# Two groups of one unit in place of one group of two, ahead of the seven-product groups of a linear-attention and bilinear-FFN kernel

## The chip, the cores and the metric

The kernel runs on one core of a Trainium2 chip. The metric is the device time of one execution in microseconds, lower is better. Four executions of the kernel before took 224.36, 224.94, 225.21 and 227.12 us; their median is 225.07 us.

## The reference

Attention with decay, causal, in blocks, for 4 batches of 8 heads, 768 positions and 64 channels; its output, with the heads side by side, is the input x (3072 x 512) of a feed-forward layer without an activation:

```python
intra = np.einsum('bhic,bhjc->bhij', qb, kb) * Dmask[None]     # lam ** (i - j) for i >= j
intra = np.einsum('bhij,bhjd->bhid', intra, vb)
inter = np.einsum('bhid,bhde->bhie', qb * lam_pow[None], kv_state)
out[:, :, sl] = intra + inter
kv_state = lam_block * kv_state + np.einsum('bhsd,bhse->bhde', kb_dec, vb)
...
a = x @ w_a                     # 512 -> 1536
b = x @ w_b
return (a * b @ w_out)          # 1536 -> 512
```

## The kernel before

**Units.** A unit is 128 positions of one batch with all heads; there are 24, six to a batch. For each unit the kernel scales q and k by powers of lam (`make_qs`, `make_ks`, so that the decay becomes a plain triangular mask), brings both into transposed form, makes the scores on TensorE and masks them on VectorE (`piece_S`, two mask operations of 128x512), adds v's outer products into a running state in PSUM and copies it out (`piece_V`, or `kv_beside` within `pieces_O`), and multiplies state and masked scores into the attention output, which ScalarE copies into the group's `xT` (`pieces_O`, lines 401 to 421).

**Groups.** The feed-forward layer runs over groups of units: `GROUPS = (4, 2, 4, 4, 4, 4, 2)`. Groups 0 and 1 use `ffn` (line 617): for each of 12 column blocks f, four matmuls into an a bank, a ScalarE copy, four matmuls into a b bank, and a VectorE product into `ab`; then 12 matmuls a unit with `wo_sb`, 512 wide. The moving operand of an a or b matmul is as wide as the group, 128 columns a unit. The groups in `S_GROUPS` (2 to 6) use `ffn_seven` (line 484): two by two blocks with seven products for eight, in six pairs of column blocks (i = 0 to 5; three fours in the last group). It needs sums of `xT` (`sums`, lines 468 to 480, on VectorE) and of the weights (`w_sums`, lines 459 to 466, "TW" in the plan, 24 VectorE operations in group 0). Of each pair, the sum `c11` goes to VectorE (line 532) where the pair is in `SUM_ON_VEC`, else to GpSimd (line 535); GpSimd always makes the product of the first half (line 545).

**Order.** The order on each engine is written by hand. While group g's feed-forward layer runs, `PLAN[g]` says at which slot the attention of later units is put in: "P" scales q and k of a unit, starts its DMA transposition (units 6 and later) and lets further q and k loads be issued on SyncE's queue (`prep_k`, `pump`); "T" transposes on TensorE (units 4 and 5); "S", "V", "O" and "O2" are the pieces above, for one or two units. Slots 0 to 11 follow the column blocks f; in group 0 each later slot follows two output matmuls, in group 1 six. In `ffn_seven`, slots are spread over the 42 steps in the same order. Engines run apart from one another and wait only for data and for buffers, so a slot fixes the order on an engine, not the time.

**Buffers.** Seven PSUM banks are handed out in turn (`ps_bank`); a matmul that starts a bank waits for the last reader of the bank's earlier content. In the output part of group 0, four are held. The k of units 4 to 9 is scaled on VectorE, everything else on GpSimd (line 260).

**Loads.** The weights come on GpSimd's queue, with the cast to bf16, and so does v (`make_vb`). v of units 4 and 5 is issued between the chunks of `w_out` (lines 761 and 762); v of a later unit is issued behind that unit's "P" (line 803). q and k of units 4 and 5 go on SyncE's queue behind small DMAs that read chunks 0 and 3 of `w_out`, and so wait for them (line 163). The outputs of the rows in the first `KEEP_GROUPS` groups (units 0 to 5) are kept in SBUF and stored in a later group ("W").

Of the kernel before, what the change touches and what calls it, by code (L numbers as in the profile page):

```python
# [22 lines left out]
def _bc(ap, dims):  # L23
# [1 line left out]
    return dataclasses.replace(ap, ap=dims)  # L25


GROUPS = (4, 2, 4, 4, 4, 4, 2)
W_CHUNKS = (256,) * 6
W_STEPS = ((0, 1), (2,), (3,), (4, 5))  # L30
W_HALVES = (4, 5)
DMA_T = range(6, 24)
KEEP_GROUPS = 2
PACK = 4


# [1 line left out]

S_GROUPS = (2, 3, 4, 5, 6)
SUM_ON_VEC = {2: (0, 1, 2, 3, 4), 3: (2, 3, 4), 4: (2, 3, 4), 5: (1, 2, 3, 4), 6: (0, 1, 2)}
PLAN = {
    0: [(0, "V", 3), (4, "TW", 0), (6, "TW", 1), (9, "TW", 2), (11, "TW", 3), (14, "TW", 4),
        (18, "TW", 5), (23, "P", 4), (26, "T", 4), (27, "P", 5), (28, "S", 4), (30, "T", 5),
        (31, "V", 4), (32, "S", 5), (34, "O2", (4, 5)), (35, "P", 6)],
    1: [(1, "P", 7), (3, "P", 8), (6, "P", 9), (7, "S", 6), (8, "V", 6), (9, "S", 7), (11, "O2", (6, 7)),
        (12, "S", 8), (12, "V", 8), (13, "S", 9), (13, "P", 10), (14, "O2", (8, 9)), (15, "P", 11)],
    2: [(1, "P", 12), (4, "P", 13), (7, "P", 14), (11, "S", 10), (11, "S", 11), (12, "P", 15),
        (14, "P", 16), (17, "P", 17)],  # L50
    3: [(6, "P", 18), (9, "P", 19), (13, "P", 20), (16, "P", 21)],
    4: [(6, "P", 22), (9, "P", 23)],
    5: [(11, "V", 22), (13, "O2", (22, 23))],
}
for _g, _u in ((2, 10), (3, 14), (4, 18)):
    PLAN[_g] += [(11, "V", _u), (13, "Q", (_u, _u + 1, _u + 2, _u + 3)), (14, "V", _u + 2),
                 (16, "O2", (_u + 2, _u + 3)), (18, "S", _u + 4), (19, "S", _u + 5)]
PLAN[2] += [(_s, "W", None) for _s in (9, 9, 9, 10, 10, 10)]


@with_exitstack
def kernel(
# [12 lines left out]
    B, H, S, D = q.shape  # L75
# [5 lines left out]
    NU = B * NB  # L81
    assert sum(GROUPS) == NU and GROUPS[0] == PACK
    KS = d_model // 128
# [60 lines left out]
    def load_w(kind, c):  # L144
        if kind == "o":
            nc.gpsimd.dma_start(out=wo_sb[:, 2 * c:2 * c + 2, :], in_=wo_r[:, 2 * c:2 * c + 2, :])
        else:
            nc.gpsimd.dma_start(out=w_part(wa_sb if kind == "a" else wb_sb, c),
                                in_=w_part(wa_r if kind == "a" else wb_r, c))

    n0 = GROUPS[0]
    pending = [("after", 0), ("q", n0), ("k", n0), ("after", 3), ("q", n0 + 1), ("k", n0 + 1), ("after", 5)]
# [100 lines left out]
    def make_vb(u):  # L253
        b, nb = divmod(u, NB)
        vb = prep_pool.tile([128, H, D], BF16, name="vb", tag="vb", bufs=8)
        nc.gpsimd.dma_start(out=vb, in_=vr[b, nb])  # L256
        U.setdefault(u, {})["vb"] = vb

    def prep_k(u):
        make_ks(u, "dve" if u < n0 + 6 else "pool")  # L260
        make_qs(u, "pool")
        used["u"] = u + 1
        if u in DMA_T:
            qkT = qkT_pool.tile([128, 2, HP, 128], BF16, name="qkT", tag="qkT")
            nc.sync.dma_start_transpose(
                out=qkT[:].rearrange("p j hp i -> p (j hp) i"),
                in_=U[u]["qk"][:].rearrange("p j h d -> p (j h d)"))
            U[u]["qT"], U[u]["kT"] = qkT[:, 0], qkT[:, 1]
        pump()

    def piece_T(u):
        d = U[u]
        tps = ps_bank("tps", [128, 2, HP, 128], BF16)
        for j in range(2):
            for hp in range(HP):
                nc.tensor.transpose(tps[:, j, hp, :], d["qk"][:, j, 2 * hp:2 * hp + 2, :], ident)
        qkT = qkT_pool.tile([128, 2, HP, 128], BF16, name="qkT", tag="qkT")
        nc.scalar.copy(qkT, tps)
        d["qT"], d["kT"] = qkT[:, 0], qkT[:, 1]
# [110 lines left out]
    def piece_S(u):  # L390
        masks(u, scores(u))

    def piece_V(u):
        kv_update(u)
        if u % NB < NB - 1:
            kv_copy(u, kv["ps"])
# [26 lines left out]

    g_u0 = [sum(GROUPS[:i]) for i in range(len(GROUPS))]
    out_r = out.rearrange("(t p) n -> t p n", p=128)
# [33 lines left out]
    def w_sums(i):  # L459
        t = tw[i] = wst_pool.tile([128, 4, 2, 256], BF16, name="tw", tag="wst")  # L460
        c = slice(256 * i, 256 * i + 256)
        a1, a2, b1, b2 = wa_sb[:, 0:2, c], wa_sb[:, 2:4, c], wb_sb[:, 0:2, c], wb_sb[:, 2:4, c]
        nc.vector.tensor_sub(t[:, 0], b1, a1)
        nc.vector.tensor_sub(t[:, 1], b2, t[:, 0])
        nc.vector.tensor_sub(t[:, 2], b2, b1)
        nc.vector.tensor_sub(t[:, 3], a2, t[:, 1])

    def sums(u):
        g = next(i for i in range(len(GROUPS)) if g_u0[i] <= u < g_u0[i] + GROUPS[i])
        if g not in S_GROUPS or u != g_u0[g] + GROUPS[g] - 1:  # L470
            return
        h = GROUPS[g] * BLK // 2
        x = xTs[u][0]
        t = wst_pool.tile([128, 4, 2, h], BF16, name="xs", tag="wst")
        x11, x12, x21, x22 = (x[:, k:k + 2, c:c + h] for c in (0, h) for k in (0, 2))
        nc.vector.tensor_add(t[:, 0], x22, x21)
        nc.vector.tensor_sub(t[:, 1], t[:, 0], x11)  # L477
        nc.vector.tensor_sub(t[:, 2], x11, x21)
        nc.vector.tensor_sub(t[:, 3], x12, t[:, 1])
        xs[g] = t  # L480

    tw, xs = {}, {}

    def ffn_seven(g, u0, n, xT, hook, last):
        h = n * BLK // 2
        nf = 512 // h
# [29 lines left out]
        def step(i, n):  # L516
# [10 lines left out]
            elif n == 2:  # L527
                p, pb = bank_of("m_p")
                product(i, p, w_of(wa_sb, 2, i), x12, True)
                d["c11"] = a_pool.tile([128, nf, h], BF16, name="c11", tag="a")  # L530
                if i in SUM_ON_VEC[g]:
                    nc.vector.tensor_add(d["c11"], d["s12"][:, 0], p)  # L532
# [28 lines left out]
        for s in range(end):  # L561
            if s in at:
                step(*at[s])
            if s % 7 == 1 and s < 42:
                hook(2 * (s // 7))
            if s % 7 == 4 and s < 35:
                hook(2 * (s // 7) + 1)
# [22 lines left out]
    def store_kept():  # L590
        row, o_sb = kept.pop(0)
        nc.sync.dma_start(out=out_r[row], in_=o_sb)

    def store(row, op, lo, hi, queue=None):
        if row < g_u0[KEEP_GROUPS]:
            if row % 2 == 0:
                keep["t"] = wst_pool.tile([128, 2, d_model], F32, name="o_kept", tag="wst")
            o_sb = keep["t"][:, row % 2, :]
            nc.scalar.copy(o_sb, op)
            kept.append((row, o_sb))  # L600
            return
        o_sb = o_pool.tile([128, d_model], F32, name="o_sb", tag="osb")
        nc.scalar.copy(o_sb[:, lo:hi], op[:, lo:hi])  # L603
        (queue or nc.sync).dma_start(out=out_r[row][:, lo:hi], in_=o_sb[:, lo:hi])
# [49 lines left out]
    def new_xT(g):  # L654
        gx[g] = xT_pool.tile([128, KS, 512], BF16, name="xT", tag="xT")
        for i in range(GROUPS[g]):
            xTs[g_u0[g] + i] = (gx[g], i * BLK)
# [100 lines left out]
                load_w(kind, c)  # L758
    for c in range(FC // 2):
        load_w("o", c)  # L760
        if c in (3, 5):
            make_vb(n0 + (c - 3) // 2)
    for u in range(2):
        kv_part(u, (0, 1))
    for u in range(2):
# [25 lines left out]
    for g, n in enumerate(GROUPS):  # L791
        if g + 1 < len(GROUPS):
            new_xT(g + 1)
        plan = {}
        for slot, name, us in PLAN.get(g, ()):
            plan.setdefault(slot, []).append((name, us))

        def hook(slot, plan=plan):
            for name, us in plan.get(slot, ()):
                if name == "P":  # L800
                    prep_k(us)
                    if us > n0 + 1:
                        make_vb(us)
                elif name == "TW":
                    w_sums(us)
                elif name == "W":
                    store_kept()
                elif name == "T":
                    piece_T(us)
                elif name == "S":  # L810
                    piece_S(us)
                elif name == "V":
                    piece_V(us)
                elif name == "O":
                    pieces_O((us,))
                elif name == "O2":
                    pieces_O(us)
                else:
                    pieces_O(us[:2], us[2:])

        if g in S_GROUPS:
            ffn_seven(g, g_u0[g], n, gx.pop(g), hook, g + 1 == len(GROUPS))
        else:
            ffn(g_u0[g], n, gx.pop(g), hook, g == 0)
# [29 lines left out]
```

## Time and profile before

The profiled execution took 224.36 us, of which the span of the core's instructions is 222.7 us. TensorE's granted clock was 1.00 throughout.

| Part of the trace | from, us | to, us |
|---|---|---|
| Loads, attention of units 0 to 3 | 0 | 17.7 |
| Group 0, column blocks | 17.7 | 38.7 |
| Group 0, output matmuls, attention of units 4 and 5 | 38.7 | 53.6 |
| Group 1 (units 4 and 5), attention of units 6 to 9 | 53.6 | 73.9 |
| Groups 2 to 5, seven products | 73.9 | 204.9 |
| Group 6 | 204.9 | 222.7 |

| Engine | busy, us | share of the span |
|---|---|---|
| TensorE (PE) | 215.0 | 97% |
| VectorE (DVE) | 146.0 | 66% |
| GpSimd (POOL) | 117.2 | 53% |
| ScalarE (ACT) | 99.7 | 45% |

A row of the timeline gives the start and the length in microseconds, the engine, the line, the operation, what is written and read, the shape, and how many were merged; in brackets stands how long the engine was idle before, and what ended that. A merged row of matmuls ends when the last one's result is out, so consecutive rows overlap; the time that TensorE really spends is read from start to start. The output rows of the page's DMA part give the median time from a DMA's issue to its landing: 5.0 us for v, 4.4 and 4.9 us for q and k, 10.2 us for a chunk of `w_out`.

### The profile page before, as it was taken

How to read it: one execution, taken by the hardware profiler on the slowest of the kernel's cores; microseconds unless marked ns; L12 is line 12 of the kernel's file. 1: busy time of each engine (PE TensorE's matmuls, PEld its weight loads, DVE VectorE, ACT ScalarE, POOL GpSimd, SP SyncE). 2: the span in 40 equal slices, each digit the busy share in tenths (PEclk: the TensorE clock that was granted, in tenths of full speed). 3: DMA queues.
4: the chain of work that ended last, by engine and by line, in shares of the span. 5: the costliest groups of instructions: out<-in, count | busy, mean ns of one | idle time of the engine just before them, and what ended most of it. 6: DMA issues, size and time to landing. Idle time of an engine off the chain costs nothing.

```text
span 222.7 us, 5228 instructions
## 1 busy us (share of the span) xinstructions
PE 215.0 (97%) x2099; PEld 146.4 (66%) x2099; DVE 146.0 (66%) x250; ACT 99.7 (45%) x182; POOL 117.2 (53%) x131
## 2 busy tenths in 40 slices
PE   7799999989999999999999999999999999999994
PEld 2475444445874788754788754788744688745974
DVE  0991685975786788893678773578773598730760
ACT  3685233028432655324556324556324556332622
POOL 6689451057346579894269992269920144600230
PEclk9999999999999999999999999999999999999999
DMA  4999999999999999999960999300911200012102
GB/s 133 267 131 172 197 205 197 199 214 199 212 222 211 206 240 107 265 288 251 238 164 18 182 219 220 121 4 17 123 51 47 97 1 3 0 47 97 47 3 94
DMA packets 98606, 31.79 MB, mean 143 GB/s; under 512 B 86551, under 2 KB 95639, under 8 KB 98583
## 3 DMA queue, kind: packets, MB, share of 16 engines
q1 hardware_dynamic: 66390, 23.53, 46.5%
q0 software_dynamic: 31904, 7.87, 38.0%
q8 instruction: 16, 0.26, 0.5%
q10 hardware_dynamic: 288, 0.07, 0.1%
q14 instruction: 8, 0.06, 0.1%
HBM read 28.32 MB, written 6.29 MB: 155 GB/s over the span
## 4 chain that ended last, share of the span: by engine, by line
PE 73%; POOL 11%; DVE 5%; issue 3%; DMA 3%; ACT 2%; SPq 1%; POOLq 0%; DVEq 0%; ACTq 0%
PE op L608 23%; PE m_q L498 14%; PE a_ps L430 7%; PE m_r L498 7%; PE b_ps L430 7%; POOL ab L545 5%; PE o_ps L324 5%; PE m_p L498 4%; POOL qk L240 3%; PE kq L290 3%; DMA k<-in_k_dram 3%; POOL vb L256 2%; PE kvd L354 1%; SPq L192 1%; ACT xT L347 1%
## 5 line engine op out<-in xcount | busy, mean ns | idle before, releaser
L608 PE MATMUL op<-wo_sb,ab 128*128 128x512 bf16 (+2 forms) x312 | 68.3, 363 | 0.6 <-POOL ab L545 0.6
L545 POOL TENSOR_TENSOR ab<-c,c 128x512 bf16<-128x512 bf16 x27 | 31.4, 1165 | 33.8 <-DVE c L543 33.4
L498 PEld LDWEIGHTS <-tw 128*128 128x128 bf16 x480 | 43.2, 98 | 6.3 <-DVE xs L477 0.2
L608 PEld LDWEIGHTS <-ab 128*128 128x128 bf16 x312 | 27.5, 98 | 27.6 <-POOL ab L545 1.6
L307 DVE TENSOR_TENSOR m<-kq,lotri 128x512 bf16<-128x512 f32 x47 | 29.8, 684 | 6.5 <-PE kq L290 5.9
L498 PE MATMUL m_q<-xs,tw 128*128 128x256 bf16 (+1 forms) x240 | 32.4, 262 | 0.0
L603 ACT COPY o_sb<-op 128x512 f32<-128x512 f32 (+2 forms) x20 | 10.9, 543 | 44.3 <-PE op L608 44.3
L240 POOL TENSOR_TENSOR qk<-qf,lp_q 128x512 bf16<-128x512 f32 x20 | 21.0, 1048 | 16.6 <-DMA qf<-in_q_dram 16.6
L535 POOL TENSOR_TENSOR c<-s 128x512 bf16<-128x512 f32 x9 | 11.4, 1269 | 31.4 <-ACT s L513 31.4
L552 DVE TENSOR_TENSOR ab<-c,m_q 128x512 bf16<-128x512 f32 x27 | 18.6, 688 | 10.6 <-PE m_q L498 8.8
L498 PEld LDWEIGHTS <-wa_sb 128*128 128x128 bf16 x240 | 21.5, 98 | 2.9
L256 POOL DMA_DIRECT2D vb<-in_v_dram x24 | 22.3, 932 | 1.2 <-DMA wa_sb<-in_moe_w_a_dram 0.6
L513 ACT COPY s<-m_q 128x512 f32<-128x512 f32 x27 | 15.8, 586 | 14.4 <-PE m_q L498 14.2
L457 DVE TENSOR_TENSOR ab<-a_sb,b_ps 128x512 bf16<-128x512 bf16 (+1 forms) x24 | 13.1, 551 | 13.6 <-PE b_ps L430 13.4
L543 DVE TENSOR_TENSOR c<-u,m_r 128x512 f32<-128x512 f32 x27 | 18.4, 681 | 5.1 <-ACT u L513 3.2
L532 DVE TENSOR_TENSOR c<-s,m_p 128x512 bf16<-128x512 f32 x18 | 12.4, 687 | 11.1 <-PE m_p L498 11.0
L439 ACT CAST a_sb<-a_ps 128x512 bf16<-128x512 f32 (+1 forms) x24 | 11.4, 479 | 17.5 <-PE a_ps L430 17.5
L430 PE MATMUL a_ps<-xT,wa_sb 128*128 128x256 bf16 (+1 forms) x104 | 18.4, 314 | 0.4 <-ACT xT L347 0.3
L549 DVE TENSOR_TENSOR c<-s,m_q 128x512 f32<-128x512 f32 x27 | 18.5, 685 | 0.5
L513 ACT COPY s<-m_r 128x512 f32<-128x512 f32 x27 | 15.9, 588 | 6.5 <-PE m_r L498 6.5
L430 PE MATMUL b_ps<-xT,wb_sb 128*128 128x512 bf16 (+1 forms) x96 | 18.4, 326 | 0.0
L513 ACT COPY u<-m_q 128x512 f32<-128x512 f32 x27 | 16.0, 593 | 5.1 <-PE m_q L498 5.1
(81 smaller groups left out, 290.0 us busy)
## 6 DMA issues: line engine op xcount, KB each, us to landing
qf<-in_q_dram SPq DMA_DIRECT2D x20, 256.0 KB, 4.4
kf<-in_k_dram SPq DMA_DIRECT2D x20, 256.0 KB, 4.9
out_dram<-o_sb SPq DMA_DIRECT2D x17, 256.0 KB, 2.0
vb<-in_v_dram POOLq DMA_DIRECT2D x24, 128.0 KB, 5.0
wa_sb<-in_moe_w_a_dram POOLq DMA_DIRECT2D x6, 256.0 KB, 7.7
wb_sb<-in_moe_w_b_dram POOLq DMA_DIRECT2D x6, 256.0 KB, 8.2
wo_sb<-in_moe_w_out_dram POOLq DMA_DIRECT2D x6, 256.0 KB, 10.2
out_dram<-o_kept SPq DMA_DIRECT2D x6, 256.0 KB, 4.1
```

The costliest lines, as they stand in the source:

```text
L240: eng_of(eng).tensor_mul(dst.rearrange("p (c b) d -> p b c d", b=2), x[:].rearrange("p (b c) d -> p b c d", b=2), lp.rearrange("p (b c) o ...
L256: nc.gpsimd.dma_start(out=vb, in_=vr[b, nb])
L307: nc.vector.tensor_mul(m, kq[i], lotri_bc)
L430: nc.tensor.matmul(ps[:, lo:hi], lhsT=w_sb[:, s, f * 128:(f + 1) * 128], rhs=xT[:, s, lo:hi], start=(s == 0), stop=(s == KS - 1), skip_gro ...
L457: nc.vector.tensor_mul(ab[:, f, :gt], a_sb[:, :gt], ps[:, :gt])
L498: nc.tensor.matmul(ps[:, f, :], lhsT=w(k, f), rhs=x[:, k, :], start=(first and f == 0 and k == 0), stop=True, skip_group_check=True)
L513: nc.scalar.copy(t, ps)
L543: nc.vector.tensor_add(c12, d["u2"], d["r"])
L545: nc.gpsimd.tensor_mul(ab[:, nf * i:nf * i + nf, 0:h], d["c11"], c12)
L549: nc.vector.tensor_add(d["c22"], d["s5"], d["q"])
L552: nc.vector.tensor_mul(ab[:, nf * i:nf * i + nf, h:2 * h], d["c22"], d["q"])
L608: nc.tensor.matmul(op[:, lo:hi], lhsT=ab[:, f, t * 128:(t + 1) * 128], rhs=wo_sb[:, f, lo:hi], start=(f == 0), stop=(f == FC - 1))
```

## The change

```diff
-GROUPS = (4, 2, 4, 4, 4, 4, 2)
+GROUPS = (4, 1, 1, 4, 4, 4, 4, 2)
...
-KEEP_GROUPS = 2
+KEEP_GROUPS = 3
...
-S_GROUPS = (2, 3, 4, 5, 6)
-SUM_ON_VEC = {2: (0, 1, 2, 3, 4), 3: (2, 3, 4), 4: (2, 3, 4), 5: (1, 2, 3, 4), 6: (0, 1, 2)}
+S_GROUPS = (3, 4, 5, 6, 7)
+SUM_ON_VEC = {3: (0, 1, 2, 3, 5), 4: (1, 3, 5), 5: (1, 3, 5), 6: (1, 2, 4, 5), 7: (0, 1, 2)}
 PLAN = {
     0: [(0, "V", 3), (4, "TW", 0), (6, "TW", 1), (9, "TW", 2), (11, "TW", 3), (14, "TW", 4),
-        (18, "TW", 5), (23, "P", 4), (26, "T", 4), (27, "P", 5), (28, "S", 4), (30, "T", 5),
-        (31, "V", 4), (32, "S", 5), (34, "O2", (4, 5)), (35, "P", 6)],
-    1: [(1, "P", 7), (3, "P", 8), (6, "P", 9), (7, "S", 6), (8, "V", 6), (9, "S", 7), (11, "O2", (6, 7)),
-        (12, "S", 8), (12, "V", 8), (13, "S", 9), (13, "P", 10), (14, "O2", (8, 9)), (15, "P", 11)],
-    2: [(1, "P", 12), (4, "P", 13), (7, "P", 14), (11, "S", 10), (11, "S", 11), (12, "P", 15),
+        (18, "TW", 5), (23, "P", 4), (26, "T", 4), (29, "S", 4), (33, "O", 4), (35, "P", 5), (35, "P", 6)],
+    1: [(0, "V", 4), (2, "T", 5), (2, "P", 7), (6, "S", 5), (8, "P", 8), (11, "P", 9), (12, "O", 5)],
+    2: [(0, "S", 6), (1, "V", 6), (4, "S", 7), (6, "P", 10), (8, "O2", (6, 7)), (9, "S", 8), (10, "V", 8),
+        (11, "P", 11), (11, "S", 9), (12, "O2", (8, 9))],
+    3: [(1, "P", 12), (4, "P", 13), (7, "P", 14), (11, "S", 10), (11, "S", 11), (12, "P", 15),
         (14, "P", 16), (17, "P", 17)],
...
     for c in range(FC // 2):
         load_w("o", c)
-        if c in (3, 5):
-            make_vb(n0 + (c - 3) // 2)
...
                 if name == "P":
                     prep_k(us)
-                    if us > n0 + 1:
-                        make_vb(us)
+                    make_vb(us)
```

The plans of the later groups are the same, each under a number that is one higher. Units 4 and 5 form a group each, so that in groups 1 and 2 an a or b matmul is 128 columns wide and there are twice as many. Unit 5's attention moves from group 0 into unit 4's group, and that of units 6 to 9 into unit 5's group. The single piece "O" makes the output of one unit with two ScalarE copies of 128x256. The same rows are kept and stored at the same place. In each seven-product group as many `c11` sums are on VectorE as before; it is other pairs, and the last pair (5) is now among them.

## The prediction

> **What bounds the kernel now.** I read the page's shares and slices first, then TensorE's timeline where the slices dip, then the other engines beside those places.
>
> ```profile
> PE 215.0 (97%) x2099; PEld 146.4 (66%) x2099; DVE 146.0 (66%) x250; ACT 99.7 (45%) x182; POOL 117.2 (53%) x131
> ...
> PE   7799999989999999999999999999999999999994
> ```
>
> TensorE is full from slice 2 to the end, but for slice 8 (44.5 to 50.1 us). So the order of TensorE's work costs its own length plus its few holes, and a change that leaves the arithmetic alone can win the holes only. The holes that this change touches lie in the end of group 0; read start to start, in TensorE's timeline:
>
> ```profile
> 45.24 0.40 PE L276 MATMUL tps<-ident,qk 128*128 128x128 bf16 x4
> 46.48 0.40 PE L276 MATMUL tps<-ident,qk 128*128 128x128 bf16 x4 [0.84 <-DVE qk L240]
> 46.71 1.03 PE L608 MATMUL op<-wo_sb,ab 128*128 128x512 bf16 x4
> 47.98 0.40 PE L290 MATMUL kq<-qkT 64*128 64x128 bf16 x8 [0.24 <-ACT qkT L278]
> ...
> 50.28 0.59 PE L608 MATMUL op<-wo_sb,ab 128*128 128x512 bf16 x2
> 50.90 0.40 PE L290 MATMUL kq<-qkT 64*128 64x128 bf16 x8
> ```
>
> A 512-wide output matmul takes 0.216 us from start to start (in the chain of waits six take 1.29), a 128-wide one 0.056 (eight take 0.45). Four transpositions from 45.24 would end at 45.46, the next start at 46.48: 1.02 us lost to unit 4's k. Four matmuls from 46.71 end at 47.57, the scores of unit 4 start at 47.98: 0.41 lost to ScalarE's copy of the transposed q and k (1012 ns). In the same way the scores of unit 5 lose 0.19 (50.71 to 50.90). Group 1's first four a matmuls take 0.87 where the next take 0.60: 0.27 lost to `xT`. Together 1.89 us.
>
> Why k of unit 4 is late is in VectorE's timeline (three rows) and GpSimd's (the last):
>
> ```profile
> 43.86 0.42 DVE L464 TENSOR_TENSOR tw<-wb_sb,tw 128x512 bf16<-128x512 bf16 x1
> 44.20 1.26 DVE L465 TENSOR_TENSOR tw<-wb_sb 128x512 bf16<-128x512 bf16 x1
> ...
> 45.73 0.69 DVE L240 TENSOR_TENSOR qk<-kf,lp_k 128x512 bf16<-128x512 f32 x1
> ```
>
> ```profile
> 44.13 1.06 POOL L240 TENSOR_TENSOR qk<-qf,lp_q 128x512 bf16<-128x512 f32 x1 [9.55 <-DMA qf<-in_q_dram]
> ```
>
> VectorE runs the weight sums without a pause from 40.48 on, and the one at 44.20, beside GpSimd's scaling of q, takes 1.26 us where its likes take 0.42. So the k scaling stands behind 24 weight sums and one collision of 0.84 us.
>
> **Unit 5's attention leaves group 0.** The scores of unit 4 move from slot 28 to 29, one more pair of matmuls (0.43) behind the transpositions, which covers the 0.41. The 0.19 goes: unit 5's transpositions come at group 1's slot 2, its scores four column blocks later (4 x 0.44 = 1.8 us, over the copy's 1.01). The 0.27 at group 1's start shrinks: the output piece of unit 4 has two slots (0.87) behind it, in which ScalarE must make two 128x256 copies (372 ns each by the `a_sb` row), with an output copy of 0.58 perhaps ahead; I keep 0.1 (0 to 0.3). Gain 0.41 + 0.19 + 0.17 = 0.77.
>
> **The 1.02 us stays, and may grow.** q and k of unit 4 should land some 1.3 to 2.6 us sooner (two v's of 0.26 MB read each, at the slices' some 200 GB/s, leave the stretch), but the 24 sums don't move. GpSimd's q scaling will hit another of them, and then, behind v's issue (0.94), unit 5's q scaling can come at 44 to 46 instead of 46.68 and hit the last ones: another 0.84. Bounds -1.02 (no collision, k in time) to +0.84; I take +0.3, nearer to one collision as seen, with half a chance of the second.
>
> **v behind its unit's scaling.** In the weights' queue v of unit 4 left at 29.86. Now it leaves behind the q scaling: GpSimd ends that at 45.19 at the latest, and the median landing for v is 5.0 us, so by 50.2. What waits for it is the first `intra` of unit 4, and behind that all of TensorE. That comes at 38.67 + 44 output matmuls (9.50) + transpositions and scores (0.45 + 0.43) + 1.02 to 1.32 + `inter` (0.2): 50.3 to 50.6. So nothing is paid, by a margin of some tenths, or more where q lands sooner. If v lands as `w_out`'s chunks do (10.2), at 55.4, the cost is 4.8. v of unit 5 has until the middle of group 1, after 58. On SyncE's queue nothing is added; unit 6's transposition, at 53.28 now, can only start sooner.
>
> **Columns of 128.** Before 96 matmuls of 256 columns, now 192 of 128, with the same weights loaded twice. The last group shows the price:
>
> ```profile
> 204.89 0.61 PE L498 MATMUL m_q<-xT,wa_sb 128*128 128x128 bf16 x8
> 205.33 0.61 PE L498 MATMUL m_r<-xs,tw 128*128 128x128 bf16 x8
> 205.78 0.61 PE L498 MATMUL m_p<-xT,wa_sb 128*128 128x128 bf16 x8
> ```
>
> Eight with eight different weights take 0.445 from start to start; four of 256 columns take 0.437 (118.01, 118.44 and 118.88 in group 3). For 24 column blocks that is 24 x 0.008 = +0.2 us.
>
> The Trainium skill ("TensorE: Matmul & The Clock Gate", Back-to-back issue gap) speaks against the split: it gives some 81 ns a matmul at 128 columns in a stream of weight loads, and calls the 56 ns of its formula too little. By that figure 192 matmuls would take an estimated 15.6 us and the change would lose 5 us; this trace's rows have 56 ns.
>
> Two single output pieces for one double one switch between state and scores once more; entering the piece costs 0.10 in the trace (52.09 to 52.19), so +0.15 (0.1 to 0.3).
>
> **Units 6 to 9 in unit 5's group.** TensorE's work there up to the last masks' use: column blocks 12 x 0.445 = 5.3, four scores 1.7, two state updates 0.4, the output piece of 6 and 7 with its state 0.93 (65.57 to 66.50 now), six output matmuls 1.3: 9.7 us. VectorE has in that time 12 products of 128x128, eight masks and three state copies:
>
> ```profile
> L307 DVE TENSOR_TENSOR m<-kq,lotri 128x512 bf16<-128x512 f32 x47 | 29.8, 684 | 6.5 <-PE kq L290 5.9 <-PE kq L712 0.2
> ...
> L457 DVE TENSOR_TENSOR ab<-a_sb,b_ps 128x256 bf16<-128x256 bf16 x12 | 5.0, 417 | 3.6 <-PE b_ps L430 3.5
> ```
>
> The 128x128 product isn't in the trace. 685 ns at 512 columns and 417 at 256 give 283 at 128, between 242 (the 128x80 product at the start) and 417. Singly, 12 x 0.283 + 8 x 0.684 + 3 x 0.684 = 10.9 us; in a row each starts some 0.09 before the last one ends (four masks in 2.48), so 9.0 when VectorE is behind. It starts 0.7 later than TensorE. So it ends at 9.7 to 11.6 against 9.7: 0 to 1.9 late. As lateness itself makes the operations run in a row, I take +0.4, near the lower end; it would show as matmuls waiting for a bank or for a mask.
>
> **Other pairs' sums.** In groups 3 and 4 TensorE loses about 0.46 each at the last pair's product on GpSimd. GpSimd's timeline in group 3:
>
> ```profile
> 117.39 1.16 POOL L545 TENSOR_TENSOR ab<-c,c 128x512 bf16<-128x512 bf16 x1 [1.83 <-DVE c L543]
> 118.50 1.05 POOL L240 TENSOR_TENSOR qk<-kf,lp_k 128x512 bf16<-128x512 f32 x1
> ...
> 126.65 1.26 POOL L535 TENSOR_TENSOR c<-s 128x512 bf16<-128x512 f32 x1
> 127.99 1.16 POOL L545 TENSOR_TENSOR ab<-c,c 128x512 bf16<-128x512 bf16 x1
> ```
>
> From 117.39 on it never rests. The sum of pair 5 (126.65) goes to VectorE, but pair 4's comes to GpSimd ahead of the second q and k scaling, in the same unbroken stretch. The last product ends where it did, at 129.15: 0. Bounds -0.9 (both holes closed) and +0.9 (doubled). In groups 2 and 5 no hole is there to close.
>
> **Sum.** -0.77 + 0.3 + 0.2 + 0.15 + 0.4 + 0 = +0.28, say +0.3 us. Against the profiled execution's 224.36 us (span 222.7) that is 224.7; that execution was the fastest of the four, and the median of 225.07 becomes 225.4 us.
>
> **Rivals.** *VectorE is the bound in unit 5's group (slower).* Its operations run singly: 1.9 us late instead of 0.4, and the group sums behind it collide with GpSimd as one does now (1.15 instead of 0.42 at 74.12), 0.7: 225.4 + 1.5 + 0.7 = 227.6. For it: 23 operations in 9.7 us. Against it: group 3 keeps VectorE as busy (9.12 of 11.8 us from 117.4) without a hole of its own. It decides once VectorE's last mask ends after TensorE's sixth output matmul of unit 5.
> *v of unit 4 is late (slower).* From a landing after 50.6 each microsecond counts in full; half of the 4.8 gives 227.8. For it: the q, k and transposition traffic of that stretch. Against it: v's of units 6 to 8 landed in 5 us in the same traffic.
> *The holes close (faster).* Unit 4's k comes in time (-1.3 against my sum) and both GpSimd holes go (-0.9): 223.2. For it: q and k land sooner. Against it: the 24 sums and GpSimd's unbroken stretch.
>
> **How the numbers follow.** About 1% (2.25 us) is what a measurement of this kernel can tell from no change. Little change: 0.6, own range 224.5 to 226.4. VectorE as the bound: 0.17. v late: 0.1. Holes closed: 0.13. The range 223.6 to 227.7 takes in the middle of each, and leaves out about a fifth. Slower by over 1% (above 227.3) gets half of the two slow rivals and a little of the rest, 0.17; faster by over 1% (below 222.8) 0.06; within 1% 0.77.
>
> **What would show it.** In the changed profile: the scores of unit 4 without a wait for ScalarE, and k's transpositions still 0.8 us or more late behind VectorE; a and b matmuls at 0.445 for eight; group 3's first product near 74 us; GpSimd's hole before the output matmuls of groups 4 and 5 unchanged. I am wrong if TensorE waits for `vb`, if a and b matmuls wait for banks for more than a microsecond in unit 5's group, or if the matmuls take 0.65 for eight.

## The result and the profile after

The changed kernel takes 227.46 us in the median of 35 executions, the kernel before 225.31 us in 56; the ratio is 1.0078, with a 95% interval of 1.0058 to 1.0098. Executions more than 1.5% above the fastest of their kernel are left out of the ratios, here and below; that takes out five of the changed kernel's 17 at a lower clock, told of further down, and the three such executions of the third experiment. So it is 1.3 to 2.2 us slower, less than 1%. The profiled execution took 226.9 us with a span of 225.2; 2.5 us more than the span before.

The page of the changed kernel, the same two lines as before:

```profile
PE 215.5 (96%) x2195; PEld 149.1 (66%) x2195; DVE 148.7 (66%) x262; ACT 101.2 (45%) x196; POOL 117.4 (52%) x131
...
PE   7898999959999999999999999999999999999994
```

TensorE has the same work (96 more, shorter matmuls), and one deep dip in place of a shallow one: the 5 in slice 8. TensorE's timeline of the changed kernel at that place:

```profile
45.74 0.39 PE L276 MATMUL tps<-ident,qk 128*128 128x128 bf16 x4
48.77 0.40 PE L276 MATMUL tps<-ident,qk 128*128 128x128 bf16 x4 [2.64 <-DVE qk L240]
49.00 1.46 PE L608 MATMUL op<-wo_sb,ab 128*128 128x512 bf16 x6
50.40 0.40 PE L290 MATMUL kq<-qkT 64*128 64x128 bf16 x8
50.72 1.90 PE L608 MATMUL op<-wo_sb,ab 128*128 128x512 bf16 x8
52.55 0.31 PE L324 MATMUL o_ps<-qkT,st 64*64 64x128 bf16 x8
52.79 0.41 PE L324 MATMUL o_ps<-m,vb 128*64 128x128 bf16 x8
...
54.01 0.39 PE L430 MATMUL a_ps<-xT,wa_sb 128*128 128x128 bf16 x4
```

Four transpositions from 45.74 end at 45.96; unit 4's k comes at 48.77. The hole is 2.81 us where it was 1.02. What follows runs without a wait of more than 0.1 us: the scores, the output piece (so v of unit 4 is there) and unit 4's group. The reason stands in VectorE's timeline (first fence) and GpSimd's (second):

```profile
41.88 1.27 DVE L465 TENSOR_TENSOR tw<-wb_sb 128x512 bf16<-128x512 bf16 x1
43.06 0.41 DVE L466 TENSOR_TENSOR tw<-wa_sb,tw 128x512 bf16<-128x512 bf16 x1
43.40 0.41 DVE L463 TENSOR_TENSOR tw<-wb_sb,wa_sb 128x512 bf16<-128x512 bf16 x1
43.85 1.28 DVE L464 TENSOR_TENSOR tw<-wb_sb,tw 128x512 bf16<-128x512 bf16 x1
...
46.51 1.26 DVE L465 TENSOR_TENSOR tw<-wb_sb 128x512 bf16<-128x512 bf16 x1
47.70 0.41 DVE L466 TENSOR_TENSOR tw<-wa_sb,tw 128x512 bf16<-128x512 bf16 x1
48.03 0.68 DVE L240 TENSOR_TENSOR qk<-kf,lp_k 128x512 bf16<-128x512 f32 x1
```

```profile
41.69 1.17 POOL L240 TENSOR_TENSOR qk<-qf,lp_q 128x512 bf16<-128x512 f32 x1 [10.52 <-DMA qf<-in_q_dram]
42.81 0.95 POOL L256 DMA_DIRECT2D vb<-in_v_dram  x1
43.78 1.05 POOL L240 TENSOR_TENSOR qk<-qf,lp_q 128x512 bf16<-128x512 f32 x1
44.77 0.94 POOL L256 DMA_DIRECT2D vb<-in_v_dram  x1
46.21 1.28 POOL L240 TENSOR_TENSOR qk<-qf,lp_q 128x512 bf16<-128x512 f32 x1 [0.50 <-DMA qf<-in_q_dram]
```

Three of GpSimd's scalings now fall into the weight sums, and three sums take 1.26 to 1.28 us; each ends some 0.3 us after the scaling beside it. The sums beside the issue of v (43.06, 43.40) keep their 0.41.

The rest of the difference is in unit 5's group. It takes 13.02 us (63.84 to 76.86). By the prediction's prices its matmuls alone need 12.07, and 12.27 with the 0.10 us that the step into each of the two output pieces costs in the profile before too. So 0.75 us are lost. Two of the waits, in TensorE's timeline, and VectorE's rows beside them (second fence):

```profile
66.91 0.40 PE L290 MATMUL kq<-qkT 64*128 64x128 bf16 x8
67.36 0.38 PE L430 MATMUL a_ps<-xT,wa_sb 128*128 128x128 bf16 x4
...
68.48 0.39 PE L430 MATMUL b_ps<-xT,wb_sb 128*128 128x128 bf16 x4
68.96 0.38 PE L430 MATMUL a_ps<-xT,wa_sb 128*128 128x128 bf16 x4
```

```profile
67.03 0.67 DVE L457 TENSOR_TENSOR ab<-a_sb,b_ps 128x128 bf16<-128x128 bf16 x3
67.62 1.28 DVE L307 TENSOR_TENSOR m<-kq,lotri 128x512 bf16<-128x512 f32 x2
```

Scores take 0.32 from start to start elsewhere (50.40 to 50.72), here 0.45; a b block takes 0.22 elsewhere, here 0.48. By the order in which `ps_bank` hands out the banks, the matmul at 67.36 waits for the first of the three products (at 0.29 us it ends at 67.32), and the one at 68.96 for the second mask (it ends at 68.90). With two smaller waits of the same sort, at 66.37 and 73.00, they sum to 0.60 us.

Put together against the profile before, from start to start: front part 0.60 (39.27 for 38.67, where TensorE's work is the same; in the profiles of the experiments that point lies between 38.3 and 40.3), from there to the first product of the seven 37.59 for 35.26 us (+2.33), from there to the end 148.34 for 148.73 (-0.39). The sum is +2.54, as the spans have it.

One thing does not show in this profile. Of the 36 executions of the changed kernel whose clock is listed, 17 have a mean granted TensorE clock of 0.991 to 0.993 and a median of 228.38 us; the other 19 have 0.998 or more and a median of 226.63. Of the 95 executions of the kernel before whose clock is listed (beside the experiments), two are at 0.992.

### The profile page after: what moved, and what is told of

Its sections match the earlier page's. It is cut to its first block, busy times and chain, and to the rows that moved or that the text cites. A ratio compares the mean times of both kernels' runs of the same rounds, so it can differ in the third digit from the quotient of the medians.

```text
span 225.2 us, 5467 instructions
## 1 busy us (share of the span) xinstructions
PE 215.5 (96%) x2195; PEld 149.1 (66%) x2195; DVE 148.7 (66%) x262; ACT 101.2 (45%) x196; POOL 117.4 (52%) x131
## 4 chain that ended last, share of the span: by engine, by line
PE 78%; POOL 6%; DVE 6%; DMA 5%; issue 2%; SPq 1%; ACT 0%; DVEq 0%; ACTq 0%
PE op L608 23%; PE m_q L498 20%; PE m_r L498 10%; PE a_ps L430 7%; PE b_ps L430 6%; PE m_p L498 5%; PE o_ps L324 4%; DMA wa_sb<-in_moe_w_a_dram 3%; POOL vb L256 2%; DMA q<-in_q_dram 2%; PE kq L290 2%; POOL ab L545 2%; POOL qk L240 2%; DVE m L307 2%; DVE tw L465 1%
## 5 line engine op out<-in xcount | busy, mean ns | idle before, releaser
L457 DVE TENSOR_TENSOR ab<-a_sb,b_ps 128x128 bf16<-128x128 bf16 (+1 forms) x36 | 14.0, 416 | 14.5 <-PE b_ps L430 10.2
L430 PE MATMUL a_ps<-xT,wa_sb 128*128 128x128 bf16 (+2 forms) x152 | 20.3, 267 | 0.7 <-DMA wa_sb<-in_moe_w_a_dram 0.6
L439 ACT CAST a_sb<-a_ps 128x128 bf16<-128x128 f32 (+1 forms) x36 | 13.2, 375 | 16.4 <-PE a_ps L430 16.3
L430 PE MATMUL b_ps<-xT,wb_sb 128*128 128x128 bf16 (+1 forms) x144 | 20.4, 272 | 0.0
```

Source lines behind the costliest of these rows:

```text
L430: nc.tensor.matmul(ps[:, lo:hi], lhsT=w_sb[:, s, f * 128:(f + 1) * 128], rhs=xT[:, s, lo:hi], start=(s == 0), stop=(s == KS - 1), skip_gro ...
L457: nc.vector.tensor_mul(ab[:, f, :gt], a_sb[:, :gt], ps[:, :gt])
```

## The experiments

Two theories stood at the start. **A**: moving v makes q and k land sooner, GpSimd's scalings meet VectorE's weight sums, and unit 4's k is late. **B**: the groups of one unit cost it, through VectorE in unit 5's group.

**1. The changed kernel with v in the weights' queue again**

```diff
         load_w("o", c)
+        if c in (3, 5):
+            make_vb(n0 + (c - 3) // 2)
...
-                    make_vb(us)
+                    if us > n0 + 1:
+                        make_vb(us)
```

> The changed kernel with v of units 4 and 5 issued between the chunks of w_out again; groups and pairs stay changed. Theory A (v's move made q and k of units 4 to 6 land sooner, so that GpSimd's scalings hit three of VectorE's weight sums instead of one): the hole before unit 4's k transpositions, 2.81 us in the changed kernel's profile, falls to about 1.0, one weight sum of 1.26 us is left, and the time falls by about 1.8 us, to a ratio of 0.999 to 1.002 to the kernel before. Theory B (the groups of one unit cost it: VectorE behind in unit 5's group): the hole may fall, but the ratio stays at 1.005 or above.

The hole is 0.98 us, one sum takes 1.15 us, and of the eight executions seven are at 0.998 or more and one at 0.985. The ratio is 1.0042 (1.0011 to 1.0072). Both theories have a part: by the middle of the intervals, which overlap, about half of the loss goes with v and about half stays with the groups.

**2. The kernel before with v moved alone**: the opposite edit, made in the kernel before.

> The kernel before with only v of units 4 and 5 moved behind its unit's scaling. Theory A: three weight sums of about 1.26 us, the hole before unit 4's k transpositions 2.5 to 2.9 us instead of 1.02, ratio 1.006 to 1.010. Theory B: ratio within 0.002 of 1.

Ratio 1.0074 (1.0039 to 1.0110); two long sums (1.23 and 1.40 us), a hole of 2.04 us, and six of twelve executions at 0.992. So there are fewer long sums than the three expected, and the hole is shorter, but v's move by itself brings a loss, and the lower clock too. The clock has the larger share here: the six executions at full clock have a median of 225.13 us, 0.6 above the kernel before in the same session (224.56), the six others 226.64 to 228.08.

**3. The changed kernel with unit 4's scaling ahead of the last four sums**

```diff
-        (18, "TW", 5), (23, "P", 4), (26, "T", 4), ...
+        (17, "P", 4), (18, "TW", 5), (26, "T", 4), ...
```

> The changed kernel with unit 4's scaling at slot 17, ahead of the last four weight sums on VectorE instead of behind them. Theory A: k is scaled some 2.2 us sooner, at about 45.8 to 46.5 us; the hole falls from 2.81 to 0.5 to 0.9 us, the masks of unit 4 follow the last weight sums without a new wait over 0.3 us, and the time falls by about 1.9 us, to a ratio of 0.998 to 1.001. Theory B: the hole falls too, but unit 5's group gives most of it back; ratio 1.004 or above.

Hole 0.83 us, ratio 1.0009 (0.9981 to 1.0037). Theory A's numbers came. But three of twelve executions are at 0.992, which a hole of 0.83 us would not explain; whether the hole was longer in those is not known, since one execution is profiled.

**4. The changed kernel with the pairs of before**: `SUM_ON_VEC` as in the kernel before, under the new group numbers.

> The changed kernel with the pairs of the kernel before in SUM_ON_VEC. Both theories: the pairs are worth nothing; GpSimd's stretch in groups 4 and 5 ends where it did, the hole of about 0.48 us before the output matmuls stays, ratio to before as the changed kernel's (1.006 to 1.010). Rival: the pairs help or harm; then the ratio differs by 0.003 or more from that.

Ratio 1.0101 (1.0072 to 1.0129), overlapping the changed kernel's; TensorE's two holes behind GpSimd's last product, before the output matmuls, are 0.46 and 0.47 us here, 0.49 and 0.48 in the changed kernel. The pairs are worth nothing that shows. Two of the six executions are at 0.992, one at 0.985. By chance the profiled one has the lower clock (0.992), and its windows show where it comes from. The columns are the stretch, its length, busy time and count of PE, PEld, DVE, ACT and POOL, the granted clock, and the DMA columns:

```profile
46.00:47.00 1.00, 0.00 (x0) 0.00 (x0) 1.00 (x4) 0.00 (x0) 0.98 (x3) 1.00 1.40 271
47.00:48.00 1.00, 0.27 (x5) 0.28 (x6) 0.67 (x2) 0.00 (x0) 1.00 (x1) 1.00 2.04 188
48.00:49.00 1.00, 1.00 (x8) 0.45 (x6) 0.00 (x0) 0.84 (x1) 1.00 (x2) 1.00 1.33 274
49.00:50.00 1.00, 1.00 (x10) 0.34 (x8) 0.00 (x0) 0.17 (x1) 0.80 (x2) 0.54 1.61 235
50.00:51.00 1.00, 1.00 (x7) 0.35 (x4) 0.80 (x2) 0.00 (x0) 1.00 (x2) 0.50 1.91 212
51.00:52.00 1.00, 1.00 (x4) 0.38 (x3) 1.00 (x2) 0.00 (x0) 0.59 (x1) 0.50 1.83 222
52.00:53.00 1.00, 0.95 (x3) 0.25 (x2) 0.69 (x2) 0.23 (x1) 0.65 (x1) 0.76 1.69 216
53.00:54.00 1.00, 0.91 (x18) 0.61 (x19) 0.00 (x0) 1.00 (x4) 1.00 (x2) 1.00 1.83 183
```

TensorE is idle through the hole (2.29 us, to 47.73), runs at full clock for another 1.3 us, and then has half the clock for 3.4 us (0.46 + 0.50 + 0.50 + 0.24 us are lost, 1.7 in all). That is the distance between the two sorts of executions, 228.38 and 226.63. So a new theory, **A2**: the hole also lets the clock drop, in half of the executions.

**5. The changed kernel with its hole filled** by matmuls on zeros, whose results nothing reads:

```diff
                 nc.tensor.transpose(tps[:, j, hp, :], ...)
+            if u == n0 and j == 0:
+                fill = ps_bank("fill", [128, 512], F32)
+                for _ in range(8):
+                    nc.tensor.matmul(fill, lhsT=idle_sb[:, :128], rhs=idle_sb, ...)
```

> The changed kernel with eight matmuls of 128x512 on zeros into a free PSUM bank between unit 4's q and k transpositions, 1.73 us that lie in the hole of 2.3 to 2.8 us. Theory A2 (a hole of over about 2 us lets the granted clock drop in half of the executions; 18 of 36 of the changed kernel have a mean clock of 0.991 to 0.993 and are some 1.7 us longer): no execution, or one, at 0.992; those at full clock unchanged at 226 to 227 us, so that the ratio to before falls from 1.008 to about 1.007 or less and none is above 228. Rival (the clock drops for another reason, as DMA traffic or the many short matmuls): half of the executions still at 0.992.

No execution of six is at 0.992 (0.998 or more). The ratio, 1.0082 (1.0049 to 1.0114), did not fall. Four of the six lie above the 226 to 227 us expected at full clock, one of them at 228.54 us, for a reason that no run shows. As the six could be luck, it was run again as the last one:

**12. The same with eleven matmuls**

> The changed kernel with eleven matmuls on zeros (2.38 us) in the hole instead of eight, so that TensorE is idle there for less than 0.5 us. Theory A2 (the hole itself lets the clock drop): no execution at 0.992, as in the six with eight; times 225 to 227.7 us, the length of the changed kernel's executions at full clock, since the wait for k is unchanged. Rival (the six were luck): about half of the executions at 0.992 and above 227.5 us.

None of seven; 225.78 to 226.95 us; ratio 1.0066 (1.0038 to 1.0093). Zero of thirteen together, against 17 of 36: the hole lets the clock drop. Filling it takes the lower clock away and leaves the wait for k, which with the cost of the groups is the larger part: at full clock the changed kernel's median is 226.63 us, where the kernel before has 224.56 to 224.88 beside the experiments.

**6. The changed kernel with eight weight sums out of group 0**

```diff
-... (11, "TW", 3), (14, "TW", 4), (18, "TW", 5), (23, "P", 4), ...
+... (11, "TW", 3), (23, "P", 4), ...
-    1: [... (11, "P", 9), (12, "O", 5)],
+    1: [... (11, "P", 9), (12, "O", 5), (12, "TW", 4)],
-    3: [(1, "P", 12), (4, "P", 13), ...
+    3: [(1, "P", 12), (2, "TW", 5), (4, "P", 13), ...
```

> The changed kernel with the last two groups of weight sums moved out of group 0: one behind unit 5's output in unit 4's group, one into group 3. Theory A: k of unit 4 is scaled by 44.5 us, no hole before its transpositions (0 to 0.3 us), no execution at 0.992; 2.5 us less than the changed kernel at full clock, ratio 0.995 to 0.999. Theory B (unit 5's group gives it back): ratio above 1.002.

A miss for the time: 1.0055 (1.0019 to 1.0092). The hole is gone, and the first product of the seven starts at 74.34 instead of 76.86. But the sums in group 3 hold VectorE up there (TensorE waits 1.26 us, to 82.26), and unit 9's scores wait 1.05 us for its DMA transposition. The edit moved the loss; it says nothing on the groups. Two of twelve are at 0.992, without a hole at unit 4 in the profiled execution, and three more took 227.57 to 228.54 us at full clock; both stay open.

**7. The kernel before with v moved, and eight weight sums in group 1** (`(2, "TW", 4)` and `(5, "TW", 5)` there, unit 4's scores at slot 29).

> The kernel before with v of units 4 and 5 moved as in the change, the last two groups of weight sums put into group 1 and the scores of unit 4 one slot later. Theory A: q and k land at 41.5 to 42.5 us and nothing stands ahead of k on VectorE; the hole of 1.02 us and the 0.41 us before the scores vanish, 1.2 to 1.6 us less than before, ratio 0.993 to 0.996. If v's move itself costs something (v late for unit 4's output), a wait of TensorE for vb shows and the ratio is 0.998 or above.

Ratio 0.9981 (0.9964 to 0.9997), the direction right, the size short. The two holes are gone, but TensorE waits for VectorE three times in group 1 (0.28, 0.54 and some 0.3 us, where the sums now lie) and 0.99 us at group 2's sums.

**8. The same with v left in the weights' queue.**

> As the run before, but with v left in the weights' queue. Theory A: k of unit 4 lands at 45.7 us, so the hole stays at about 1.0 us, now ended by the DMA, and only the 0.41 us before the scores goes: ratio 0.997 to 0.999. Rival (only the weight sums held k back, the landing didn't): the hole vanishes here too, ratio 0.993 to 0.996.

Ratio 1.0003 (0.9984 to 1.0023), above the 0.997 to 0.999 expected and further still from the rival's 0.993 to 0.996. VectorE waits 2.84 us for k of unit 4, whose scaling starts at 46.47: the landing is the limit then, as theory A has it. The hole is 0.25 us instead of the 1.0 expected, because this execution reached the output matmuls late (40.27).

**9. The changed kernel with unit 4's scaling ahead of the last eight sums**

```diff
-... (14, "TW", 4), (18, "TW", 5), (23, "P", 4), (26, "T", 4), ...
+... (13, "P", 4), (14, "TW", 4), (18, "TW", 5), (26, "T", 4), ...
```

> The changed kernel with unit 4's scaling at slot 13, ahead of the last eight weight sums. Theory A: k is scaled at 43 to 44.5 us, the hole before its transpositions is 0 to 0.3 us, no execution drops to 0.992; what stays is unit 5's group, where VectorE and the landing of unit 9's transposition cost 0.5 to 1.3 us. Ratio 0.998 to 1.002. Rival (unit 5's group costs nothing): 0.992 to 0.996.

Ratio 1.0019 (0.9994 to 1.0044), 225.38 us in the median, no execution of twelve below 0.999. The sums still collide (1.35 and 1.29 us), but nothing on TensorE waits for them. Unit 9's scores do wait, in TensorE's timeline:

```profile
68.69 0.39 PE L430 MATMUL b_ps<-xT,wb_sb 128*128 128x128 bf16 x4
69.71 0.40 PE L290 MATMUL kq<-qkT 64*128 64x128 bf16 x8 [0.63 <-DMA qkT<-qk]
```

**10. The kernel before with v moved, unit 4's scaling at slot 13, and the last sums where VectorE waits anyway**

```diff
-... (14, "TW", 4), (18, "TW", 5), (23, "P", 4), (26, "T", 4), (27, "P", 5), (28, "S", 4), ... (35, "P", 6)],
+... (13, "P", 4), (26, "T", 4), (27, "P", 5), (28, "TW", 4), (29, "S", 4), ... (35, "P", 6), (35, "TW", 5)],
```

> The kernel before with v of units 4 and 5 moved, unit 4's scaling at slot 13, and the last two groups of weight sums where VectorE waits anyway in the seventh run: one behind unit 5's scaling, one behind unit 6's. The hole of 1.02 us and the 0.41 us before the scores go and group 1 gets no weight sums, so its waits of 0.28, 0.54 and 0.41 us go as well: 1.0 to 1.5 us less than before, ratio 0.993 to 0.996. If the weight sums collide with GpSimd's scaling there and hold up masks or k: 0.997 or above.

Ratio 0.9972 (0.9953 to 0.9991), 224.19 us in the median: faster than both kernels, by less than hoped. In its TensorE timeline the transpositions of q and k are one row, and the scores follow without a wait for ScalarE:

```profile
44.95 0.61 PE L276 MATMUL tps<-ident,qk 128*128 128x128 bf16 x8
45.39 1.46 PE L608 MATMUL op<-wo_sb,ab 128*128 128x512 bf16 x6
46.78 0.40 PE L290 MATMUL kq<-qkT 64*128 64x128 bf16 x8
```

0.48 and 0.46 us are given back in group 1, to a state copy on VectorE and to a DMA transposition. It has the groups of two where run 9 has the groups of one, and the front is mended in both, though the last eight sums and the pairs lie elsewhere: 1.0019 against 0.9972, some 1.0 us (0.4 to 1.8 by the two intervals), is what the groups of one cost. Run 1 against the kernel before, where groups and pairs alone differ, says 0.0042, about the same.

**11. The changed kernel with q and k of unit 5 behind the last chunk of `w_out`**, an edit that only moves a landing:

```diff
-("after", 3), ("q", n0 + 1), ("k", n0 + 1), ("after", 5)]
+("after", 3), ("after", 5), ("q", n0 + 1), ("k", n0 + 1)]
```

> The changed kernel with q and k of unit 5 behind the last chunk of w_out instead of the fourth, which only moves their landing, from 43.4 to some 46 us. Theory A: GpSimd's scalings of units 5 and 6 come after or at the end of the weight sums; one or two sums of 1.26 us instead of three, hole 1.0 to 1.9 us instead of 2.3 to 2.8, at most a quarter of the executions at 0.992, ratio 1.001 to 1.005. If the long sums have another cause than GpSimd's scaling, hole and ratio stay (2.3 to 2.8 us, 1.008).

Ratio 1.0055 (1.0034 to 1.0076), one of twelve at 0.992. VectorE's long sums (first fence) and GpSimd's scalings (second):

```profile
42.55 1.15 DVE L464 TENSOR_TENSOR tw<-wb_sb,tw 128x512 bf16<-128x512 bf16 x1
...
45.42 1.27 DVE L466 TENSOR_TENSOR tw<-wa_sb,tw 128x512 bf16<-128x512 bf16 x1
46.61 0.68 DVE L240 TENSOR_TENSOR qk<-kf,lp_k 128x512 bf16<-128x512 f32 x1
```

```profile
42.38 1.03 POOL L240 TENSOR_TENSOR qk<-qf,lp_q 128x512 bf16<-128x512 f32 x1 [10.53 <-DMA qf<-in_q_dram]
...
45.11 1.29 POOL L240 TENSOR_TENSOR qk<-qf,lp_q 128x512 bf16<-128x512 f32 x1 [0.79 <-DMA qf<-in_q_dram]
...
48.67 1.03 POOL L240 TENSOR_TENSOR qk<-qf,lp_q 128x512 bf16<-128x512 f32 x1 [1.38 <-DMA qf<-in_q_dram]
```

The third scaling comes after the sums; two sums are long, and the hole is 1.83 us. Over the profiles with unit 4's k behind all sums the hole follows the count: one long sum 1.0 us (before, run 1), two 1.8 to 2.3 (runs 2, 4 and 11), three 2.8 to 3.0 (the changed kernel, and runs 5 and 12 with the fill counted in).

## Why the prediction was right or wrong

The forecast was +0.3 us and little change; measured are +1.3 to +2.2 us by the ratio, still under 1%. The two main mechanisms were named, their sizes were off, and a third cost was not in the sum. That the median of 227.46 us still lies within the stated range is in part luck: the range reached to 227.7 for two rivals, v late and VectorE as the bound, neither of which came at its price, and the own range of "little change" ended at 226.4.

**The 1.02 us that "stays, and may grow"** is the step that failed. Its bounds were -1.02 to +0.84 and its value +0.3; it measured +1.79, outside. The prediction counted one collision for certain and half a second one, from units 4 and 5. There are three: unit 6's scaling, at 48.46 before, comes at 46.21. Each collision also stretches the run of sums by 0.85 us, so that it is still going when the next q lands; without any, the sums would have ended at some 45.5 (48.03 less three times 0.85), ahead of unit 6's scaling. The prediction held the sums' end fixed while it moved the landings.

**The granted clock** was not in the sum at all. After a hole of this length it costs another 1.7 us in about half of the executions, and lifts the median of all from 226.63 (full clock alone) to 227.46.

**VectorE in unit 5's group**: +0.4 taken, 0.75 measured (13.02 against 12.27), within the bounds of 0 to 1.9, and seen as the waits for banks that were named (0.60 us, under the microsecond set as the sign of being wrong). So this rival was half right: VectorE is late there. The argument against it, that group 3 keeps VectorE as busy, did not hold by the prediction's own figures: 9.12 of 11.8 us there is 77%, 9.0 in 9.7 is 93%. But the second part of its price, the collision in the group's sums (0.7), did not come; these sums took 0.42 each this time, which is part of the 0.39 us won behind 76.86.

**What was right.** The forecast of 0.77 for the waits of 0.41, 0.19 and 0.27 us was near: 0.67 is won. Two of them were read too large, since each holds the 0.10 us that the step into the scores costs without any wait, and that stays (57.80 to 57.90 now, 67.80 to 67.90 before). The 128-column matmuls take 0.44 to 0.45 us for eight (54.68, 55.13, 55.57), as the last group's rows said: +0.2 us, and nothing of the 81 ns of the Trainium skill's page. The single output pieces take 0.59 and 0.58 us against 0.92 for the double one, +0.25 for +0.15. v was in time: no wait for it in the changed kernel's groups. The pairs of `SUM_ON_VEC` are worth nothing that shows, and the two holes behind GpSimd stay (0.49 and 0.48). With the measured sizes the same sum is -0.67 + 1.79 + 0.2 + 0.25 + 0.75 = +2.32, and the timeline has +2.33.

What stays open: how the 1.0 us that the groups of one cost divides between VectorE's lateness and unit 9's transposition, which becomes late as soon as the front is mended (0.5 to 1.1 us in runs 1, 3, 6 and 9); the lower clock in runs 3 and 6; and the executions of runs 5 and 6 over 227.5 us at full clock.

## What to carry to other kernels

A load that is taken out of a crowded stretch makes its neighbours land sooner, and what they release on another engine may land on top of the work that is on the path; ask for every earlier landing what it starts, and beside what. When two engines hold each other up, recompute the end of the stretch after each collision before asking which one is the next. A hole in TensorE's work may cost more than its own length, as those of 2.0 to 2.8 us did here in about half of the executions, so look at the granted clock of many executions, not at one profile.

## What the runs showed of the hardware

A VectorE sum of two operands in SBUF took 1.15 to 1.6 us beside a GpSimd scaling instead of 0.42, ended some 0.3 us after it in the changed kernel, and was not held up by GpSimd's issue of a DMA (0.94 us). The Trainium skill ("SBUF — State Buffer", Who interferes with whom) states that a VectorE operation with both inputs in SBUF contends with a GpSimd operation that reads SBUF, that the one which issues first has the shared port to itself, and that the other stands still. The traces agree that one of the two is held up to the end of the other. Which one, the start times do not tell: in runs 3, 4 and 5 a sum that had started 0.26 to 0.28 us ahead of the scaling was the one held (1.61 to 1.62 us), and the scaling took its usual 1.05. VectorE's row and GpSimd's in run 4:

```profile
44.78 1.62 DVE L464 TENSOR_TENSOR tw<-wb_sb,tw 128x512 bf16<-128x512 bf16 x1
```

```profile
45.05 1.05 POOL L240 TENSOR_TENSOR qk<-qf,lp_q 128x512 bf16<-128x512 f32 x1
```

In the one profile that shows it (run 4), the granted clock fell to half for 3.4 us, and began to fall some 1.3 us after TensorE had work again. The Trainium skill ("TensorE: Matmul & The Clock Gate", Part 1) tells of a half-rate state after an idle window of about 3.4 us, on windows that run freely. The depth and the length agree; but the idle time here was 2.0 to 2.8 us, not 3.4, and about half of the executions fell.
